# Linear attention beside a Mish layer: the two softmax planes of a head laid side by side, the queries' minus plane weighted before the product with kv, softmax sums on GpSimd, and an order of steps written as a list

## The chip, the cores and the metric

The kernel runs on one core of one Trainium2 chip. The metric is device time in microseconds (us) of one execution, the median of several runs, and lower is better. Inside a core five engines run their own instruction streams and wait for each other by semaphores: TensorE (PE, matrix products; its weight loads are listed apart as PEld), VectorE (DVE), ScalarE (ACT), GpSimd (POOL) and SyncE (SP, which here issues most DMAs). Products land in PSUM, which is eight banks of 128 partitions by 512 fp32 numbers; everything else lies in SBUF. GpSimd works on SBUF only in this kernel.

## The reference, cut to what matters

```python
x = A_x                                  # (1, 2048, 512) bf16
xn = layernorm(x)
q, k, v = split(xn @ wqkv)               # 32 heads of 16 columns each
pq, pk = q @ w_phi[head], k @ w_phi[head]
phi_q = concat(softmax(pq), softmax(-pq))    # over the 16 columns of a head: 32 columns
phi_k = concat(softmax(pk), softmax(-pk))
kv  = phi_k^T @ v                        # per head 32 x 16, summed over all 2048 rows
z   = sum over rows of phi_k             # per head 32
o   = (phi_q @ kv) / (phi_q @ z + 1e-6)
h   = xn @ w1 + b1                       # 512 -> 1792
out = x + o @ wo + mish(h) @ w2          # 1792 -> 512
```

The first softmax of a row is called the plus plane, the one of the negated logits the minus plane. No row maximum has to be kept: exp(p - max) and exp(min - p) are formed, and each plane's sum over its 16 columns divides it.

## The kernel before, in words

**Tiling.** The 2048 rows are 16 tiles of 128 rows, taken in 4 groups of 4 tiles. The Mish layer's hidden columns are 14 blocks of 128. `hidden` makes one unit: 4 matmuls of 512 columns (L178), then the Mish activation on ACT (L185); 14 units per group, 56 in all. `second_layer` (L400) makes 14 matmuls for one tile of 128 rows and leaves the sum open in PSUM; `project_out` (L409) adds 4 matmuls of o @ wo to the same sum; `residual` (L417) adds x on DVE and writes the tile out.

**The attention steps.** `fold` multiplies w_phi into the weights, so that `logits` (4 matmuls, L156) gives pk or pq directly. A stage s runs over one group: stages 0 to 3 are the keys of the four groups, stages 4 to 7 the queries. For each stage:

- `logits` makes the four tiles' logits, copied out of PSUM to `p_sb` by ACT or DVE (L196).
- `extremes` on DVE takes maximum and minimum over the 16 columns in a tree of four TENSOR_TENSOR instructions (L209 three times, L215), and subtracts (L220). It does so for the plus plane and then for the minus plane. The result is the tile `e`, of which there are two buffers.
- `exponentials` on ACT: exp over two of the four tiles at a time (L230).
- for the keys, `normalise` on DVE: TENSOR_REDUCE sums 16 columns (L248), RECIPROCAL (L256), a copy that doubles each factor (L257), and one multiplication of the whole of e (L261). Then `accumulate`: e^T @ [v, 1] on TensorE, 32 matmuls per group with 129 columns each (L284): a stationary block is one plane of 8 heads (128 columns), the moving one 128 columns of v and a column of ones.
- for the queries, e is turned by DMA (`turn`) without being normalised, and `attend` multiplies each plane with its masked kv: 8 matmuls of 144 columns per tile (L328), 128 columns of numerators, 8 of denominators and 8 of plain plane sums. ACT copies the result out of PSUM in four pieces (L337 to L344). `combine` on DVE (L360 to L385) then works out, from the two planes' sums and denominators, the factor of each plane, multiplies both planes' numerators (2048 columns for a pair of tiles), adds the two planes, and turns the result by DMA for `project_out`.

**The order.** The kernel is recorded under a manual schedule: each engine executes its instructions in the order in which the Python code issues them, and waits are put in where data or a buffer isn't ready. The order is written out by hand in the loops from L499 and from L567. SP issues nearly all DMAs in that order too, the transposes among them.

**LayerNorm** takes statistics on DVE (L116, L118) and the power -1/2 on POOL (L119, L122). The application (L128) runs on DVE for groups 0 and 1 and on POOL for groups 2 and 3.

**PSUM** has five banks for all products of 512 columns (`ps`), and three for one tile that holds kv or an `attend` result in turn (`ps2`).

The lines that the steps of the prediction rest on:

```python
rhs=vext[g % 2][:, i, j, 0:129]            # L287, accumulate
rhs=kvm[:, pl, j, :]                               # L331, attend, 144 columns
engine = nc.gpsimd if t0 > TPG else nc.vector      # L126, ln_apply
ps  = ctx.enter_context(tc.tile_pool(name="ps", bufs=5, ...))    # L59
```

Of the kernel before, what the change touches and what calls it, by code (L numbers as in the profile page):

```python
# [9 lines left out]
FP32 = mybir.dt.float32  # L10
# [3 lines left out]
AX = mybir.AxisListType  # L14


@with_exitstack
def kernel(
# [40 lines left out]
    ps = ctx.enter_context(tc.tile_pool(name="ps", bufs=5, space=bass.MemoryType.PSUM))  # L59
# [5 lines left out]
    kvm = persist.tile([P, 2, 4, 144], BF16, name="kvm")  # L65
# [14 lines left out]
    KVmask = consts.tile([P, 136], FP32, name="KVmask")  # L80
    vext = [vpool.tile([P, TPG, 4, 136], BF16, name=f"vext{i}") for i in range(2)]
# [11 lines left out]
    def fold(wT, dst, dve):  # L93

        for kt in range(KT):
            pf = ps.tile([P, 512], FP32, name="pfold", tag="mm")
            for j in range(4):
                nc.tensor.matmul(
                    pf[:, j * P : (j + 1) * P],
                    lhsT=wT[:, j, kt * P : (kt + 1) * P],  # L100
                    rhs=Wbd[:, j, :],
                    start=True,
                    stop=True,
                )
            if kt in dve:
                nc.vector.tensor_copy(dst[:, kt, :], pf[:])
            else:
                nc.scalar.copy(dst[:, kt, :], pf[:])
# [16 lines left out]
    def ln_apply(t0, n, mv, rstd, xn, at):  # L125
        engine = nc.gpsimd if t0 > TPG else nc.vector  # L126
        for i in range(n):
            engine.tensor_scalar(  # L128
                out=xn[:, at + i, :],
                in0=x_sb[:, t0 + i, :],  # L130
                scalar1=mv[:, i, 0:1],
                scalar2=rstd[:, i : i + 1],
                op0=ALU.subtract,
                op1=ALU.mult,
            )
# [26 lines left out]
    def value(t, copy):  # L162
        keep(t, project(wv, t), copy)

    def keep(t, pv, copy):
        copy(
            vext[(t // TPG) % 2][:, t % TPG, :, 0:128], pv.rearrange("p (j c) -> p j c", j=4)
        )

    units = iter([(g, f) for g in range(NG) for f in range(FT)])  # L170

    def hidden(n):

        for _ in range(n):
            g, f = next(units)
            ph = ps.tile([P, 512], FP32, name="ph", tag="mm")
            for kt in range(KT):
                nc.tensor.matmul(  # L178
                    ph[:],
                    lhsT=w1_sb[:, kt, f * P : (f + 1) * P],  # L180
                    rhs=xnT[:, g * TPG : (g + 1) * TPG, kt, :],
                    start=(kt == 0),
                    stop=(kt == KT - 1),
                )
            nc.scalar.activation(  # L185
                acts[:, f, g * 512 : (g + 1) * 512], ph[:], ACT.Mish, bias=b1f[:, f : f + 1]
            )
# [4 lines left out]
    def logits(s, i, copy):  # L192
        if i == 0:
            p_of[s] = smx.tile([P, TPG, 512], BF16, name="p_sb", bufs=1)
        pp = project(wkp if s < NG else wqp, (s % NG) * TPG + i)
        copy(p_of[s][:, i, :], pp)  # L196

    def extremes(s, between=None):

        e = epool.tile([P, TPG, 2, 512], BF16, name="e")  # L200
        e_of[s] = e
        pv = p_of.pop(s)[:].rearrange("p t (c e) -> p (t c) e", e=16)
        for pl, op in enumerate((ALU.max, ALU.min)):
            if pl == 1 and between is not None:
                between()
            src = pv
            for half in (8, 4, 2):
                m = smx.tile([P, 128, half], BF16, name=f"m{half}", bufs=1)
                nc.vector.tensor_tensor(  # L209
                    out=m[:], in0=src[:, :, 0:half], in1=src[:, :, half : 2 * half], op=op  # L210
                )
                src = m[:]

            m = smx.tile([P, 128, 1, 2], BF16, name="m1", bufs=1)
            nc.vector.tensor_tensor(out=m[:, :, 0, :], in0=src, in1=src[:, :, ::-1], op=op)  # L215
            mb = m[:].rearrange("p (t c) u o -> p t c u o", t=TPG).to_broadcast(
                [P, TPG, 32, 8, 2]
            )
            p5 = pv.rearrange("p (t c) (e o) -> p t c e o", t=TPG, o=2)
            nc.vector.tensor_tensor(  # L220
                out=e[:, :, pl, :].rearrange("p t (c e o) -> p t c e o", e=8, o=2),
                in0=p5 if pl == 0 else mb,
                in1=mb if pl == 0 else p5,
                op=ALU.subtract,
            )

    def exponentials(s, ks=(0, 1)):
        for k in ks:
            v = e_of[s][:, 2 * k : 2 * k + 2, :, :]
            nc.scalar.activation(v, v, ACT.Exp)  # L230
            if s >= NG:
                turn(s, k)

    def turn(s, k):

        qT = epool.tile([P, 2, 8, P], BF16, name="qT", bufs=3)
        qT_of[2 * (s - NG) + k] = qT
        for i in range(2):
            nc.sync.dma_start_transpose(
                out=qT[:, i, :, :],  # L240
                in_=e_of[s][:, 2 * k + i, :, :].rearrange("p l c -> p (l c)"),
            )

    def normalise(s, k, between=None):

        v = e_of[s][:, 2 * k : 2 * k + 2, :, :]
        t = smx.tile([P, 128], FP32, name="s")
        nc.vector.reduce_sum(  # L248
            t[:], v.rearrange("p t l (c e) -> p (t l c) e", e=16), axis=AX.X
        )  # L250
        if between is not None:
            between()
        r = smx.tile([P, 128], BF16, name="r")
        r2 = smx.tile([P, 128, 2], BF16, name="r2")
        with nc.allow_low_precision("the softmaxes are bf16"):
            nc.vector.reciprocal(r[:], t[:])  # L256
        nc.vector.tensor_copy(  # L257
            r2[:], r[:].rearrange("p (c o) -> p c o", o=1).to_broadcast([P, 128, 2])
        )
        vv = v.rearrange("p t l (c e o) -> p (t l c) e o", e=8, o=2)  # L260
        nc.vector.tensor_tensor(  # L261
            out=vv, in0=vv, in1=r2[:, :, None, :].to_broadcast([P, 128, 8, 2]), op=ALU.mult
        )

    def blocks(kv, pl, j, width):

        bank, at = (pl, j) if j < 3 else (2, pl)
        return kv[:, bank, at * 144 : at * 144 + width]

    def by_parts(kv, c0, c1):  # L270

        v = kv[:, :, 0:432].rearrange("p b (k c) -> p b k c", c=144)
        return v[:, 0:2, :, c0:c1], v[:, 2, 0:2, c0:c1]
# [3 lines left out]
    def accumulate(g):  # L277
        if g == 0:
            kv_of[0] = ps2.tile([P, 3, 512], FP32, name="pkv", tag="kv")
        e = e_of.pop(g)  # L280
        for j in range(4):
            for pl in range(2):
                for i in range(TPG):
                    nc.tensor.matmul(  # L284
                        blocks(kv_of[0], pl, j, 129),
                        lhsT=e[:, i, pl, j * P : (j + 1) * P],
                        rhs=vext[g % 2][:, i, j, 0:129],  # L287
                        start=(g == 0 and i == 0 and (j == 0 or (j == 3 and pl == 0))),
                        stop=(g == NG - 1 and i == TPG - 1),
                        skip_group_check=True,  # L290
                    )

    def mask_kv():
        a, b = by_parts(kv_of[0], 0, 128)
        nc.vector.tensor_tensor(
            out=kvm[:, :, 0:3, 0:128], in0=a,
            in1=KVmask[:, None, None, 0:128].to_broadcast([P, 2, 3, 128]), op=ALU.mult,
        )
        nc.vector.tensor_tensor(
            out=kvm[:, :, 3, 0:128], in0=b,  # L300
            in1=KVmask[:, None, 0:128].to_broadcast([P, 2, 128]), op=ALU.mult,
        )
        a, b = by_parts(kv_of[0], 128, 129)
        for pl in range(2):
            nc.vector.scalar_tensor_tensor(
                out=kvm[:, pl, 0:3, 128:136], in0=a[:, pl].to_broadcast([P, 3, 8]), scalar=5e-7,
                in1=KVmask[:, None, 128:136].to_broadcast([P, 3, 8]),
                op0=ALU.add, op1=ALU.mult,
            )
        nc.vector.scalar_tensor_tensor(  # L310
            out=kvm[:, :, 3, 128:136], in0=b.to_broadcast([P, 2, 8]), scalar=5e-7,
            in1=KVmask[:, None, 128:136].to_broadcast([P, 2, 8]), op0=ALU.add, op1=ALU.mult,
        )

    nd_of, oT_of, po_of, tmp_of = {}, {}, {}, {}

    def attend(h, i):

        if i == 0:
            nd_of[h] = (  # L320
                (wkp, wv)[h % 2][:].rearrange("p (i l) c -> p i l c", i=2),
                opool.tile([P, 2, 2, 2, 4, 8], FP32, name="ds"),
            )
        nm, ds = nd_of[h]
        pnd = ps2.tile([P, 3, 512], FP32, name="pnd", tag="kv")
        for pl in range(2):
            for j in range(4):
                nc.tensor.matmul(  # L328
                    blocks(pnd, pl, j, 144),
# [294 lines left out]
```

## Time and profile before

| | |
|---|---|
| time, median of 3 runs | 183.61 us (183.5 to 183.72) |
| span of the profiled execution, first to last instruction | 181.8 us; the page gives no time of its own for this execution beside the span |
| TensorE | busy 175.2 us (96%), 1024 matmuls, granted clock 1.00 |
| VectorE | busy 146.6 us (81%), 255 instructions |
| ScalarE | busy 126.3 us (69%), 194 instructions, 13 of them table loads of 1.283 us |
| GpSimd | busy 24.9 us (14%), nothing after 54.5 us |
| DMA | 18.02 MB, queue 1 busy for 40.5% of 16 engines' span |

How it is read: "busy" is the time in which an engine had an instruction running; a row of the groups gives line, engine, operation, tile names, shapes and a count, then busy us and mean ns of one, then the idle time just before and what ended it. The chain of work in order of time starts at the last instruction and goes back, at each step, to what released it; printed forwards it gives start, length and what ran. On that chain TensorE stands for 73%, VectorE for 18%. Lengths in the chain are from start to start, so they are the price of an instruction in a full stream, where the mean ns of a group also holds what overlaps the next instruction.

### The profile page before, as it was taken

The page shows a single profiled execution, that of the slowest core. Times are in us where ns is not written, and L with a number is a line of the kernel's source. Part 1 is how long each engine was busy: PE and PEld are TensorE (multiplying, and loading weights), DVE is VectorE, ACT ScalarE, POOL GpSimd, SP SyncE. Part 2 cuts the span into 40 slices and gives each one's busy share as a digit, 9 for nine tenths or more (in the row PEclk, how much of TensorE's full clock was granted, in tenths as well). Part 3 has the DMA queues.
Part 4 walks back from the last instruction along what each step waited for, and adds up shares of the span by engine and source line. Part 5 has one row for each costly group of instructions (what it writes and reads, how often), then busy time and mean ns, then how long its engine had stood idle before and what let it go on. Part 6 is the DMA issues. An engine that isn't in the chain of part 4 may idle for free.

```text
span 181.8 us, 2744 instructions
## 1 busy us (share of the span) xinstructions
PE 175.2 (96%) x1024; PEld 90.1 (50%) x1039; DVE 146.6 (81%) x255; ACT 126.3 (69%) x194; POOL 24.9 (14%) x30
## 2 busy tenths in 40 slices
PE   6899999999899999999999999999999999999993
PEld 2454344464344654644464555555554545455561
DVE  2989979999999799989998883399916997647963
ACT  2367999988998899979978999272842557235300
POOL 4403079301990000000000000000000000000000
PEclk9999999999999999999999999999999999999999
DMA  6997896300027100000001903933079302990633
GB/s 146 293 401 263 179 356 157 60 4 2 0 58 153 24 0 0 0 0 4 0 0 27 192 16 60 190 96 63 0 171 204 87 5 42 200 192 30 73 104 115
DMA packets 44393, 18.02 MB, mean 99 GB/s; under 512 B 36828, under 2 KB 43868, under 8 KB 44380
## 3 DMA queue, kind: packets, MB, share of 16 engines
q1 hardware_dynamic: 43408, 17.50, 40.5%
q10 hardware_dynamic: 972, 0.35, 0.7%
q8 instruction: 8, 0.13, 0.3%
q14 instruction: 5, 0.04, 0.1%
HBM read 6.84 MB, written 2.10 MB: 49 GB/s over the span
## 4 chain that ended last, share of the span: by engine, by line
PE 73%; DVE 18%; ACT 3%; issue 2%; DMA 2%; DVEq 0%
PE po L400 26%; PE ph L178 17%; PE pproj L156 14%; PE po L409 7%; PE pnd L328 4%; DVE stats L116 4%; PE pkv L284 3%; DVE m L209 3%; DVE s L248 2%; ACT e L230 2%; DVE e L220 2%; DMA x_sb<-in_A_x_dram 2%; DVE e L261 2%; DVE xn L128 1%; DVE r L256 1%
## 5 line engine op out<-in xcount | busy, mean ns | idle before, releaser
L400 PE MATMUL po<-w_sb,acts 128*128 128x512 bf16 (+1 forms) x232 | 50.0, 366 | 0.3
L178 PE MATMUL ph<-xnT,w_sb 128*128 128x512 bf16 x224 | 49.5, 379 | 0.6 <-ACT p_sb L196 0.6
L185 ACT ACTIVATE acts<-ph,b1f 128x512 bf16<-128x512 f32 x56 | 35.2, 696 | 2.6 <-PE ph L178 2.5
L178 PEld LDWEIGHTS <-w_sb 128*128 128x128 bf16 x224 | 21.8, 98 | 26.8 <-issue 0.9
L230 ACT ACTIVATE e<-e 128x2048 bf16<-128x2048 bf16 x16 | 30.1, 1906 | 6.7 <-DVE e L220 6.6
L400 PEld LDWEIGHTS <-acts 128*128 128x128 bf16 x238 | 22.9, 98 | 22.2
L156 PEld LDWEIGHTS <-xnT 128*128 128x128 bf16 x192 | 18.3, 98 | 21.6 <-DMA xnT<-xn 0.8
L417 DVE TENSOR_TENSOR x_sb<-po,x_sb 128x512 bf16<-128x512 f32 (+1 forms) x17 | 10.6, 654 | 12.6 <-PE po L409 12.6
L196 ACT CAST p_sb<-pproj 128x512 bf16<-128x512 f32 x25 | 14.0, 586 | 9.6 <-PE pproj L156 9.6
L248 DVE TENSOR_REDUCE s<-e 128x128 f32<-128x2048 bf16 x8 | 18.2, 2275 | 1.9 <-ACT e L230 1.9
L128 POOL TENSOR_SCALAR xn<-x_sb,mv,rstd 128x512 bf16<-128x512 bf16 x8 | 16.6, 2086 | 0.2
L156 PE MATMUL pproj<-wv,xnT 128*128 128x512 bf16 x62 | 14.8, 379 | 0.1
L156 PE MATMUL pproj<-wqk,xnT 128*128 128x512 bf16 x63 | 14.4, 379 | 0.1
L409 PE MATMUL po<-wqk,ob 128*128 128x512 bf16 (+1 forms) x65 | 14.3, 366 | 0.1
L337 ACT CAST wkp<-pnd 128x768 bf16<-128x768 f32 x8 | 6.4, 804 | 10.5 <-PE pnd L328 6.5
L209 DVE TENSOR_TENSOR m<-m 128x512 bf16<-128x512 bf16 (+1 forms) x32 | 11.5, 359 | 1.1
L156 PE MATMUL pproj<-wkp,xnT 128*128 128x512 bf16 x49 | 11.7, 379 | 0.1
L209 DVE TENSOR_TENSOR m<-p_sb 128x1024 bf16<-128x1024 bf16 x16 | 11.0, 685 | 1.0 <-ACT p_sb L196 1.0
L337 ACT CAST wv<-pnd 128x768 bf16<-128x768 f32 x8 | 6.4, 794 | 7.3 <-PE pnd L328 5.1
L328 PEld LDWEIGHTS <-qT 128*128 128x128 bf16 x128 | 9.1, 98 | 3.8
L116 DVE BATCH_NORM_STATS2 stats<-x_sb 128x6 f32<-128x512 bf16 x16 | 10.0, 678 | 1.2 <-DMA x_sb<-in_A_x_dram 1.2
L261 DVE TENSOR_TENSOR e<-e,r 128x2048 bf16<-128x2048 bf16 x8 | 10.7, 1337 | 0.3
(67 smaller groups left out, 179.4 us busy)
## 6 DMA issues: line engine op xcount, KB each, us to landing
w_sb<-in_B_w_dram SPq DMA_DIRECT2D x2, 1792.0 KB, 8.6
out_dram<-x_sb SPq DMA_DIRECT2D x15, 128.0 KB, 1.8
x_sb<-in_A_x_dram SPq DMA_DIRECT2D x1, 1024.0 KB, 11.4
x_sb<-in_A_x_dram SPq DMA_DIRECT2D x1, 512.0 KB, 3.9
wv<-in_A_wqkv_dram SPq DMA_DIRECT2D x1, 512.0 KB, 4.7
wqk<-in_A_wo_dram SPq DMA_DIRECT2D x1, 512.0 KB
x_sb<-in_A_x_dram SPq DMA_DIRECT2D x1, 256.0 KB, 3.2
x_sb<-in_A_x_dram ACTq DMA_DIRECT2D x1, 256.0 KB, 3.5
```

The source lines that it names most:

```text
L116: nc.vector.bn_stats(stats[:, i, :], x_sb[:, t0 + i, :])
L128: engine.tensor_scalar(out=xn[:, at + i, :], in0=x_sb[:, t0 + i, :], scalar1=mv[:, i, 0:1], scalar2=rstd[:, i : i + 1], op0=ALU.subtract, ...
L156: nc.tensor.matmul(pp, lhsT=xnT[:, t, kt, :], rhs=w[:, kt, :], start=(kt == 0), stop=(kt == KT - 1),)
L178: nc.tensor.matmul(ph[:], lhsT=w1_sb[:, kt, f * P : (f + 1) * P], rhs=xnT[:, g * TPG : (g + 1) * TPG, kt, :], start=(kt == 0), stop=(kt == ...
L185: nc.scalar.activation(acts[:, f, g * 512 : (g + 1) * 512], ph[:], ACT.Mish, bias=b1f[:, f : f + 1])
L209: nc.vector.tensor_tensor(out=m[:], in0=src[:, :, 0:half], in1=src[:, :, half : 2 * half], op=op)
L230: nc.scalar.activation(v, v, ACT.Exp)
L248: nc.vector.reduce_sum(t[:], v.rearrange("p t l (c e) -> p (t l c) e", e=16), axis=AX.X)
L261: nc.vector.tensor_tensor(out=vv, in0=vv, in1=r2[:, :, None, :].to_broadcast([P, 128, 8, 2]), op=ALU.mult)
L328: nc.tensor.matmul(blocks(pnd, pl, j, 144), lhsT=qT_of[h][:, i, pl * 4 + j, :], rhs=kvm[:, pl, j, :], start=True, stop=True,)
L400: nc.tensor.matmul(po[:, c], lhsT=acts[:, f, t * P : (t + 1) * P], rhs=w2_sb[:, f, c], start=(f == 0), stop=False,)
L409: nc.tensor.matmul(po[:, c], lhsT=oT_of[h][:, t % 2 * 4 + j, :], rhs=wo_sb[:, j, c], start=False, stop=(j == 3),)
```

## The change

Five things change at once, and the head (everything up to the logits of the first group) stays but for the names.

1. **Planes side by side.** The tile e is now [tile, 8 blocks, 2 planes, 64 columns]. A block is 4 heads, with both planes: 2 x 4 x 16 = 128 rows for the product. The moving operand of `accumulate` is then 64 columns of v and a column of ones, 65 in all, where there were 129; that of `attend` is 64 numerators and 4 denominators, 68 where there were 144. The number of matmuls is unchanged. One product now sums over both planes.
2. **The minus plane weighted first** (`weigh`, for the queries). So that one product can sum both planes, the minus plane is multiplied by (sum of the plus plane) / (sum of the minus plane) ahead of the DMA that turns e. Numerator and denominator then carry the same factor. `combine` shrinks to a reciprocal, a doubling copy and one multiplication of 1024 columns, and the four copies out of PSUM become two (`gather`).
3. **Sums on GpSimd** (`sums`). Fifteen of sixteen half-stages (two tiles each) are summed by four additions on GpSimd, over 1024, 512, 256 and 128 columns, with fp32 between. The eight of the queries are new, as the queries had no sums of their own; one of these (S 6 0) is a TENSOR_REDUCE on DVE. In three places GpSimd also makes the doubling copy.
4. **LayerNorm's application** runs on DVE for all groups.
5. **A new order**, written as a list of steps that the code executes one by one, with copies out of PSUM separated from the product that they empty, and with DVE (v), ACT (a) or GpSimd (p) named for each. PSUM is six banks for the products and two for kv or `attend`.

In the list: LN statistics, AP apply and turn (two tiles), L / LC logits and their copy, WL logits into the wide PSUM tile, V / VC values and copy, H / M hidden unit and Mish, E a plane of extremes, X exponentials, S sums, R reciprocal and doubling, N normalise, A accumulate (two tiles), KV mask, W weigh and turn, Q attend, G gather, C combine, O second layer, P project out, Y residual, F / FC fold and copy, LD late weight loads, WT the turned query weights.

```diff
+STEPS = """
+LN 1; V 0; V 2; H 0; VC 2 a; H 1; M 0; M 1; H 2; H 3; H 4; M 2; H 5; H 6; M 3; M 4; M 5; E 0 0; E 0
+1; M 6; H 7; H 8; M 7; H 9; H 10; M 8; M 9; AP 1 0; H 11; H 12; H 13; M 10; M 11; M 12; M 13; AP 1
+1; LN 2; LN 3; V 1; L 1 0; VC 0 v; WL 1; X 0 0; V 3; L 1 3; VC 1 a; H 14; AP 2 0; AP 2 1; X 0 1; AP
+3 0; S 0 0 p; LC 1 0 v; LC 1 3 a; V 5; VC 3 a; LC 1 1 v; H 15; M 14; AP 3 1; WL 2; M 15; VC 5 a; LC
+1 2 v; E 1 0; H 16; H 17; V 4; M 16; M 17; H 18; M 18; H 19; M 19; H 20; H 21; M 20; M 21; VC 4 v; S
+0 1 p; H 22; H 23; M 22; M 23; E 1 1; R 0 0 p; V 7; VC 7 v; X 1 0; V 6; L 2 0; LD; L 2 3; WT; R 0 1
+v; L 2 2; S 1 0 p; LC 2 0 v; LC 2 3 a; L 2 1; LC 2 2 a; X 1 1; F 0; FC 0 a; S 1 1 p; H 24; M 24; VC
+6 v; H 25; N 0 0; H 26; H 27; N 0 1; A 0 0; H 28; A 0 1; H 29; M 25; M 26; M 27; H 30; M 28; LC 2 1
+v; E 2 0; F 1; H 31; M 29; V 11; R 1 0 p; M 30; E 2 1; M 31; H 32; M 32; L 3 0; F 2; X 2 1; S 2 1 p;
...
+VC 14 a; LC 5 2 a; LC 5 1 a; X 4 1; L 5 3; LC 5 3 v; L 6 1; A 3 0; A 3 1; E 5 0; S 4 1 p; H 49; H
+50; M 49; M 50; H 51; M 51; H 52; H 53; H 54; M 52; W 4 0; E 5 1; M 53; M 54; L 6 0; O 1; KV; X 5 0;
+Q 0 0; G 0 0; L 6 3; LC 6 0 a; LC 6 1 v; H 55; W 4 1; LC 6 2 v; Q 0 1; G 0 1; C 0; O 2; O 3; LC 6 3
...
+3; P 6; P 7; S 6 1 p; W 6 1; Q 5 0; S 7 0 p; Y 5; W 7 0; O 11; G 5 0; Y 6; Y 7; Q 5 1; O 12; G 5 1;
+Q 6 0; O 13; C 4; C 5; G 6 0; Q 6 1; P 8; P 9; S 7 1 p; G 6 1; W 7 1; Q 7 0; P 10; Y 8; Y 9; Y 10; C
+6; P 11; G 7 0; Q 7 1; G 7 1; O 14; O 15; P 12; P 13; C 7; P 14; Y 11; Y 12; Y 13; Y 14; P 15; Y 15
+"""
...
-    ps = ctx.enter_context(tc.tile_pool(name="ps", bufs=5, space=bass.MemoryType.PSUM))
+    ps = ctx.enter_context(tc.tile_pool(name="ps", bufs=6, space=bass.MemoryType.PSUM))
...
-        engine = nc.gpsimd if t0 > TPG else nc.vector
+        engine = nc.vector
...
+    def sums(s, k, pooled=False):
+
+        t = smx.tile([P, 128], FP32, name="s")
+        s_of[s, k] = t
+        src = pair(s, k).rearrange("p t j l (c e) -> p (t j l c) e", e=16)
+        if not pooled:
+            nc.vector.reduce_sum(t[:], src, axis=AX.X)
+            return
+        for half in (8, 4, 2, 1):
+            h = smx.tile([P, 128, half], FP32, name=f"h{half}", bufs=1)[:] if half > 1 else t[:, :, None]
+            nc.gpsimd.tensor_tensor(
+                out=h, in0=src[:, :, 0:half], in1=src[:, :, half : 2 * half], op=ALU.add
+            )
+            src = h
...
+    def weigh(s, k):
+
+        t = s_of.pop((s, k))[:].rearrange("p (t l c) -> p t l c", l=2, c=4)
+        r = smx.tile([P, 16, 4], FP32, name="q")
+        r2 = smx.tile([P, 16, 4, 2], BF16, name="q2")
+        nc.vector.reciprocal(r[:], t[:, :, 1, :])
+        nc.vector.tensor_tensor(
+            out=r2[:], in0=t[:, :, 0, :, None].to_broadcast([P, 16, 4, 2]),
+            in1=r[:, :, :, None].to_broadcast([P, 16, 4, 2]), op=ALU.mult,
+        )
+        vv = pair(s, k).rearrange("p t j l c -> p (t j) l c")[:, :, 1, :].rearrange(
+            "p t (c e o) -> p t c e o", e=8, o=2
+        )
+        nc.vector.tensor_tensor(
+            out=vv, in0=vv, in1=r2[:, :, :, None, :].to_broadcast([P, 16, 4, 8, 2]), op=ALU.mult
+        )
+        turn(s, k)
...
+                    blocks(kv_of[0], j, 65),
+                    lhsT=e[:, i, j, :, :].rearrange("p l c -> p (l c)"),
+                    rhs=vext[g % 2][:, i, j, 0:65],
...
+                blocks(pnd, j, 68), lhsT=qT_of[h][:, i, j, :], rhs=kvm[:, j, :],
...
+    for step in STEPS.split(";"):
+        name, *args = step.split()
+        run[name](*(int(a) if a.isdigit() else a for a in args))
```

More of the change, by code (lines that the diff above doesn't have):

```diff
@@ L160, in project, with value, keep @@
         return pp
-    def value(t, copy):
-        keep(t, project(wv, t), copy)
-    def keep(t, pv, copy):
+    pv_of, ph_of, pl_of = {}, {}, {}
+    def value(t):
+        pv_of[t] = project(wv, t)
+    def keep(t, copy):
         copy(
-            vext[(t // TPG) % 2][:, t % TPG, :, 0:128], pv.rearrange("p (j c) -> p j c", j=4)
-        )
[L170 to L186, printed above, removed]
-            )
+            vext[(t // TPG) % 2][:, t % TPG, :, 0:64],
+            pv_of.pop(t).rearrange("p (j c) -> p j c", j=8),
+        )
@@ L190, with logits, take @@
     p_of, e_of, qT_of = {}, {}, {}
-    def logits(s, i, copy):
+    def logits(s, i, pp=None):
+        pl_of[s, i] = project(wkp if s < NG else wqp, (s % NG) * TPG + i, pp)
+    def take(s, i, copy):
         if i == 0:
             p_of[s] = smx.tile([P, TPG, 512], BF16, name="p_sb", bufs=1)
[L195 to L217, printed above, removed]
-            )
[L219 to L225, printed above, removed]
@@ L275 @@
-    kv_of = {}
[L277 to L291, printed above, removed]
@@ L471 @@
     ln_apply(0, 2, *st0, xn, 0)
-    fold(wT, wkp, (3,))
+    for kt in range(KT):
+        fold(wT, kt)
+        unfold(wkp, kt, (act, act, act, dve)[kt])
     ln_turn_pe(0, xn, 0, dve)
@@ L477 @@
     ln_apply(2, 2, *st1, xn, 2)
-    logits(0, 0, act)
+    logits(0, 0)
+    take(0, 0, act)
     for i in range(2, 4):
@@ L548 @@
[L548 to L593 removed]
+        logits(0, i)
@@ new lines, with wide @@
+    wide_of = {}
+    def wide(i):
+        if i == 1:
+            wide_of[0] = ps2.tile([P, 2, 512], FP32, name="pwide", tag="kv")
+        logits(1, i, wide_of[0][:, i - 1, :])
+    wT_of = {}
+    run = {
+        "LN": stats, "AP": apply, "LD": load_late, "WL": wide,
+        "L": logits, "LC": lambda s, i, c: take(s, i, copies[c]),
+        "V": value, "VC": lambda t, c: keep(t, copies[c]),
+        "H": hidden, "M": mish,
+        "E": extremes, "X": exponentials, "S": lambda s, k, c: sums(s, k, c == "p"),
+        "R": lambda s, k, c: invert(s, k, c == "p"), "N": normalise, "A": accumulate,
+        "KV": mask_kv, "W": weigh, "Q": attend, "G": gather, "C": combine,
+        "O": second_layer, "P": project_out, "Y": residual,
+        "WT": lambda: wT_of.update({0: load_turned(0)}),
+        "F": lambda kt: fold(wT_of[0], kt), "FC": lambda kt, c: unfold(wqp, kt, copies[c]),
+    }
```

395 lines of the change are left out of this document (162 added, 233 removed).

## The prediction

> **What bounds the kernel now.** I read the page's engine list first, then the waits of TensorE, then the chain of waits in order of time, then the groups with shapes kept apart.
>
> The engine list:
>
> ```profile
> PE 175.2 (96%) x1024; PEld 90.1 (50%) x1039; DVE 146.6 (81%) x255; ACT 126.3 (69%) x194; POOL 24.9 (14%) x30
> ```
>
> TensorE has work for nearly the whole span, and the waits view shows that it hardly ever waits once started:
>
> ```profile
> PE warm L457 <- POOL ident masks.py:199: 1.4, 1, 1.4
> PE ph L178 <- ACT p_sb L196: 0.6, 1, 0.6
> PE ptr L140 <- DVE wkp L106: 0.5, 1, 0.5
> ```
>
> The chain in order of time (start, length, what) gives the price of each kind of product in a full stream:
>
> ```profile
> 58.95 1.81 PE pkv L284 x32
> ...
> 67.67 0.89 PE pfold L98 x16
> ...
> 84.19 8.63 PE ph L178 x40
> ...
> 102.84 0.50 PE pnd L328 x8
> ```
>
> A product of 512 columns costs 0.2158 us (8.63/40), of 129 columns 0.0566 (1.81/32), of 128 columns 0.0556 (0.89/16), of 144 columns 0.0625 (0.50/8). So from 8.5 us to 177.8 us the kernel is a gapless stream of products; what shortens it is fewer TensorE nanoseconds, provided no other engine is late.
>
> The last view is the timeline of DVE and POOL where LayerNorm runs on POOL beside DVE's normalise (each POOL instruction is 2.08 us, the lines merge two):
>
> ```profile
> 29.36 4.16 POOL L128 TENSOR_SCALAR xn<-x_sb,mv,rstd 128x512 bf16<-128x512 bf16 x2
> ...
> 29.56 1.67 DVE L261 TENSOR_TENSOR e<-e,r 128x2048 bf16<-128x2048 bf16 x1
> ```
>
> ```profile
> 50.32 4.13 POOL L128 TENSOR_SCALAR xn<-x_sb,mv,rstd 128x512 bf16<-128x512 bf16 x2
> ...
> 53.64 1.23 DVE L261 TENSOR_TENSOR e<-e,r 128x2048 bf16<-128x2048 bf16 x1
> ```
>
> The same DVE multiplication takes 1.23 us where it starts 1.2 us into a POOL instruction, and 1.67 where it starts 0.2 us after one began (the same at 48.42, behind the POOL start at 48.22). POOL's own time doesn't move. DVE loses 0.44 us to POOL's start, about until POOL has read its 512 columns (0.64 us).
>
> **Narrower products.** 128 matmuls of 129 columns become 65, 128 of 144 become 68; before, 128 x 0.0566 + 128 x 0.0625 = 15.24 us. Low end: the straight line through 512 and 129 columns is 0.4157 ns per column plus 3.0 ns, so 30.0 and 31.2 ns, 7.83 us, 7.4 saved. High end: nothing is gained below the narrowest row, 55.6 ns each, 14.23 us, 1.0 saved (each product needs its own weight load, which no row shows alone in a stream). The rows at 128, 129, 144 and 512 columns lie on one line with no sign of a floor, so I take the line plus 8 ns for weight loads no longer fully covered: 38.5 ns, 9.86 us, **5.4 saved**. All other products stay in number and width.
>
> The Trainium skill ("TensorE: Matmul & The Clock Gate", section "Back-to-back issue gap") gives N/2.4 + 2.5 ns, but says that it leaves out the weight load. By it the saving would be 7.5 us and the time 179.5; the four rows above agree with it to 0.4 ns, and nothing here shows 65 columns.
>
> **The head's end.** Due times from here on are the rows' lengths added along the list, from the end of the first logits at 12.87 us. The list puts two values (V 0, V 2) ahead of the first hidden unit, where there were four. So H 0 is due at 12.87 + 8 x 0.2158 = 14.6; w1's load is issued at 5.9 and lands 9.1 us later, at 15.0. **+0.4**. X 0 0 moves back by some 6 us (before 22.84; now behind 14 Mish units, due 28.7), and the whole of the keys' softmax with it; that is covered by group 0's hidden units, which now all stand ahead. SP: w2 and wo are issued behind six xnT transposes instead of two (about 32.5 instead of 20.1), the turned query weights behind these; with 8.2 us for w2 and 4.7 for a turned load they land at about 45, and F 0 is due at 47.8, O 0 at 87. Nothing.
>
> **ACT.** Copies of `attend`: before 0.80 + 0.38 + 0.26 + 0.22 = 1.66 us per tile, now 0.22 + 0.59: 16 x 0.85 = -13.6. Seven logits copies, the wide copy of 1.43, a value and two folds go to DVE, about -7. Two more table loads, +2.6. ACT falls to about 108 us. No gain of its own, as it wasn't the bound.
>
> **DVE.** Off: seven of eight sums of 2.275 us, -15.9; `combine` from 29.7 (its rows added) to 8 x (0.553 + 0.226 + 0.692) = 11.8, -17.9; three doublings, -1.0; kv's mask, about -0.9. On: 8 `weigh` at 0.553 + 0.292 + 0.692, +12.3; LayerNorm's other 8 tiles at 0.343, +2.7; 13 more copies out of PSUM at 0.68, +8.8. Net -12, to about 135 us. The total is no problem; the place is.
>
> **POOL.** It loses 16.6 us of LayerNorm and gets 15 sums of 1920 columns. No row has an addition there. Low end from the 128-column memset, 0.205 us, 1.6 ns per column, 3.1 us a sum; high end from TENSOR_SCALAR, 2.086/512 = 4.07 ns, 7.8 us. Nearest to small plain work are the selects, 293 and 344 ns for 128 columns, so 2.5 ns: **4.8 us a sum**, 72 in all. A TENSOR_REDUCE is done in 2.3, so each softmax is 2.5 us later; the list leaves room for that, as A s stands far behind X s.
>
> **What is late next: DVE between E 1 0 and E 5 1.** E 1 0 can start at 35.3 (WL 2 made and copied), as TensorE ends WL 2 at 34.9. DVE's steps from there to E 5 1 add up to 60.8 us: ten planes of extremes at 2.97, eight N at 1.25, the rest copies, reciprocals and one W. E 5 1 is due at 105.6: it releases X 5 0 (1.82), behind which on ACT stands G 0 0 (0.75), which empties PSUM for Q 0 1, due on TensorE at 108.2. So 105.6 - 35.3 - 60.8 = 9.5 us of room. But e has two buffers: E 2 0, E 3 0, E 4 0 and E 5 0 wait until A 0 1, A 1 1, A 2 1 and A 3 1 have run on TensorE, and what is lost behind such a wait isn't won back before it. I count 6 of the 9.5 as useful.
>
> Into this stretch fall eight sums, 32 POOL additions. Two-input work (planes and N, 40 of 60.8 us) takes two thirds of DVE's time, so about 20 additions meet it. Bounds for one meeting: 0, as at 53.64, and 1.2 us, a whole addition (4.8/4). I take the measured 0.44: 8.8 us, less 6, **+3 us** of TensorE waiting, mostly where ACT's exponentials hold up copies behind them (VC 8 behind X 2 0, LC 4 2 behind X 3 0). If POOL were free of cost, 0; if 1.2, 24 less at most 9.5: 14.5.
>
> **Behind E 5 1** DVE has some 50 us of work in 70 and is led by TensorE. W ahead of `turn` adds a sum and 1.6 us between exp and the turned queries; S 5 1 to Q 3 0 has 128.7 - 115.2 = 13.5 us for 4.8 + 1.6 + about 4 of SP and DMA. Last, Q 7 1 ends some 7.8 us before P 14, and G, C 7 and its transpose take 0.8 + 1.6 + 1.2 + 3.1 = 6.7: covered by 1 us. Behind the last product nothing changes.
>
> **The sum.** -5.4 + 0.4 + 3.0 = -2.0. The span of 181.8 becomes 179.8. The timed runs have 183.61 as median, 1.8 above the profiled span; I leave that as it is: **181.6 us**.
>
> **Rivals.**
>
> *A. DVE and POOL shut each other out.* Place: the stretch above. If every two-input DVE instruction waits for the whole of the addition that it meets, TensorE loses 14.5 to 18 us: 183.6 - 5.0 + 14.5 to 18 = 193 to 197, I say 194. It decides from (5.0 + 6)/20 = 0.55 us a meeting, barely above the 0.44 seen. For it: POOL read 512 columns in 0.64 us, an addition reads twice its columns, so the first of a sum would read for 2.6 us. Against it: the instruction at 29.56 did not wait out the 1.88 us that POOL's had left.
>
> The Trainium skill ("SBUF — State Buffer", section "Who interferes with whom") says that a VectorE instruction with two SBUF inputs and a GpSimd one that reads SBUF exclude each other for a whole instruction. By that rule this rival is the outcome. The trace agrees that they meet, and not on the length: 1.67 us where the rule would make it 3.1.
>
> *B. Narrow products are no cheaper than 128 columns.* 1.0 saved: 183.6 - 1.0 + 0.4 + 3.0 = 186.0. For it: one weight load of 98 ns per product; against it: the line.
>
> *C. POOL is dear, 7.8 us a sum.* Then S 4 1 ends near 109, W 4 1 and LC 6 2 behind it release O 2 some 2.7 us late, and A 3 1, P 2 and Q 3 0 lose about 2.5 more: 181.6 + 3 to 5 = 185.
>
> *D. Nothing collides*: 183.6 - 5.4 + 0.4 = 178.6, and 176.6 with the line's full saving.
>
> **How the numbers follow.** Forecast and D together, one mechanism with meetings from 0 to 0.55 us, 0.51, own range 176.6 to 183.5; A 0.30; B 0.11; C 0.08. A measurement tells 0.2% (0.37 us) from no change. Of the 0.51, 0.49 are faster and 0.02 the same; of B and C 0.02 the same; the rest, 0.47, slower, and I put 0.01 of that at the same for A's lower edge. Range 176.6 to 194: outside are A's upper half and a little below.
>
> **What would show it.** The products of 65 and 68 columns in the chain: 38 ns (30 to 56). The waits of TensorE: near zero outside 50 to 110 us, about 3 us inside, ended by ACT. POOL's rows of L296: 2.5, 1.3, 0.6, 0.3 us. The planes' rows on DVE (685, 425, 292, 292, 1225 ns before): means up by a few tens of ns in the forecast, by hundreds in A. X 5 0 at about 105. The forecast is wrong if DVE's two-input means double, or if narrow products show more than 50 ns.

## The result, and the profile after

The changed kernel takes 196.87 us (median of 4 runs, 196.23 to 197.38), the kernel before 183.67 in the same session. The ratio is 1.0711, 95% interval 1.0683 to 1.0739: 13.2 us slower. The forecast of 181.6 us was wrong in sign and the time lies above the range's upper end of 194.0. It is what rival A gives (193 to 197).

The engine list of the changed kernel, and three rows of its 40 slices (busy tenths; PEclk is the granted clock in tenths):

```profile
PE 173.2 (89%) x1023; PEld 83.9 (43%) x1039; DVE 167.5 (86%) x247; ACT 113.2 (58%) x153; POOL 88.1 (45%) x85
...
PE   7899999999699989785996993999499999799993
...
DVE  2989993799999999999998999699999999992814
...
PEclk9999999999789999999999997899999999999999
```

TensorE is busy 2 us less than before in a span 12.7 us longer (194.5 against 181.8). DVE was forecast at 135 us and shows 167.5. The granted clock falls twice, each time at a gap in the PE row; at the other gaps it stays. The chain that ended last has turned over. Before, TensorE had 73% of it and VectorE 18%; now:

```profile
DVE 56%; PE 31%; ACT 6%; issue 4%; DMA 2%; POOL 0%; DVEq 0%; POOLq 0%; ACTq 0%
```

POOL holds 0% of that chain, and DVE waited for a sum of POOL's only once, for 0.4 us. So it is not POOL's sums that come late. The groups of DVE with shapes kept apart (count, busy us, mean ns of one, then idle time) show where the 32 us went:

```profile
L248 DVE TENSOR_TENSOR m<-p_sb 128x1024 bf16<-128x1024 bf16 x16 | 16.2, 1012 | 0.4
L257 DVE TENSOR_TENSOR e<-p_sb,m 128x2048 bf16<-128x2048 bf16 x8 | 12.4, 1544 | 0.6
L248 DVE TENSOR_TENSOR m<-m 128x512 bf16<-128x512 bf16 x16 | 11.8, 736 | 0.6
...
L248 DVE TENSOR_TENSOR m<-m 128x256 bf16<-128x256 bf16 x16 | 10.3, 642 | 0.6
...
L257 DVE TENSOR_TENSOR e<-m,p_sb 128x2048 bf16<-128x2048 bf16 x8 | 9.8, 1225 | 0.3
...
L237 DVE CAST p_sb<-pproj 128x512 bf16<-128x512 f32 x11 | 7.5, 682 | 0.6 <-PE pproj L192 0.6
```

The same operations took 685, 1225, 425, 292, 1225 and 676 ns before. The four rows shown that grew all read two inputs in SBUF, and each grew by 311 to 350 ns. The second subtraction (e<-m,p_sb) did not, but it never meets an addition: in this order it always starts with POOL idle. Copies out of PSUM did not grow either, and they do meet: one at 49.82, beside an addition begun at 49.83, took 0.68 us.

One place in the timeline shows the mechanism. POOL's additions and DVE's tree at the start of the prediction's stretch (start, length, instruction; x2 merges two):

```profile
35.73 2.64 POOL L296 TENSOR_TENSOR h<-e 128x1024 f32<-128x1024 bf16 x1
38.45 2.03 POOL L296 TENSOR_TENSOR h<-h 128x512 f32<-128x512 f32 x2
```

```profile
35.70 0.69 DVE L248 TENSOR_TENSOR m<-p_sb 128x1024 bf16<-128x1024 bf16 x1
36.42 3.51 DVE L248 TENSOR_TENSOR m<-m 128x512 bf16<-128x512 bf16 x2
```

DVE started first, at 35.70, and ran its usual 0.69 us; POOL's addition, started 0.03 us later, took 2.64 us instead of the 2.13 it takes alone (at 31.12). Then DVE's next instruction waited until that addition was over: in the chain it stands with 2.24 us, where it needs 0.43. So the engines wait for each other to the end of the instruction, whichever came first. The rest of the trace agrees: 48 DVE instructions are longer by more than 0.05 us than the same rows of the run without sums (e2, below), and in each the extra time is what the POOL instruction running at its start had left, less 0.13 to 0.15 us. In 47 of the 48 that POOL instruction is an addition, in one a copy.

The waits of TensorE, its wait at the very start left out:

```profile
PE pnd L387 <- DVE kvm L373: 3.1, 1, 3.1
PE po L442 <- ACT p_sb L237: 2.6, 1, 2.6
PE ph L214 <- DVE p_sb L237: 2.3, 1, 2.3
PE pkv L356 <- DVE e L317: 2.3, 1, 2.3
PE pproj L192 <- ACT p_sb L237: 1.9, 1, 1.9
...
PE pnd L387 <- DMA qT<-e: 1.2, 1, 1.2
```

These six are 13.4 us, where the kernel before had 1.1 behind its start. Three end on a DVE step and two on a copy of ScalarE.

### The profile page after: what moved, and what is told of

Same layout as the page of the kernel before. It is cut to its first block, busy times and chain, and to the rows that moved or that the text cites. A ratio compares the mean times of both kernels' runs of the same rounds, so it can differ in the third digit from the quotient of the medians.

```text
span 194.5 us, 2775 instructions
## 1 busy us (share of the span) xinstructions
PE 173.2 (89%) x1023; PEld 83.9 (43%) x1039; DVE 167.5 (86%) x247; ACT 113.2 (58%) x153; POOL 88.1 (45%) x85
## 4 chain that ended last, share of the span: by engine, by line
DVE 56%; PE 31%; ACT 6%; issue 4%; DMA 2%; POOL 0%; DVEq 0%; POOLq 0%; ACTq 0%
DVE m L248 18%; DVE e L257 10%; PE ph L214 8%; PE po L442 8%; PE pproj L192 6%; DVE m L254 4%; PE po L450 3%; DVE e L335 3%; ACT e L272 3%; PE warm L496 3%; DVE q L328 3%; DVE p_sb L237 2%; DVE r L309 2%; DVE x_sb L458 2%; DVE e L317 2%
## 5 line engine op out<-in xcount | busy, mean ns | idle before, releaser
L214 PE MATMUL ph<-xnT,w_sb 128*128 128x512 bf16 x224 | 53.6, 390 | 3.2 <-DVE p_sb L237 2.3
L296 POOL TENSOR_TENSOR h<-e 128x1024 f32<-128x1024 bf16 x15 | 33.4, 2226 | 45.5 <-ACT e L272 31.5
L296 POOL TENSOR_TENSOR h<-h 128x512 f32<-128x512 f32 (+1 forms) x30 | 34.4, 1147 | 2.4
L192 PEld LDWEIGHTS <-xnT 128*128 128x128 bf16 x192 | 18.6, 99 | 25.9 <-issue 4.7
L248 DVE TENSOR_TENSOR m<-m 128x512 bf16<-128x512 bf16 (+1 forms) x32 | 22.0, 689 | 1.1
L458 DVE TENSOR_TENSOR x_sb<-po,x_sb 128x512 bf16<-128x512 f32 (+1 forms) x17 | 10.7, 653 | 8.5 <-PE po L450 8.5
L248 DVE TENSOR_TENSOR m<-p_sb 128x1024 bf16<-128x1024 bf16 x16 | 16.2, 1012 | 0.4
L237 ACT CAST p_sb<-pproj 128x512 bf16<-128x512 f32 x19 | 10.8, 587 | 8.1 <-PE pproj L192 4.3
L450 PE MATMUL po<-wqk,oT 128*128 128x512 bf16 (+1 forms) x65 | 14.7, 366 | 0.2
L401 ACT COPY ds<-pnd 128x32 f32<-128x32 f32 x16 | 2.9, 184 | 18.8 <-PE pnd L387 18.8
L192 PE MATMUL pproj<-wkp,xnT 128*128 128x512 bf16 x55 | 13.2, 379 | 0.2 <-DVE xnT L179 0.2
L257 DVE TENSOR_TENSOR e<-p_sb,m 128x2048 bf16<-128x2048 bf16 x8 | 12.4, 1544 | 0.6
L296 POOL TENSOR_TENSOR s<-h 128x128 f32<-128x128 f32 x15 | 10.8, 717 | 1.2
```

The source lines that it names most:

```text
L192: nc.tensor.matmul(pp, lhsT=xnT[:, t, kt, :], rhs=w[:, kt, :], start=(kt == 0), stop=(kt == KT - 1),)
L214: nc.tensor.matmul(ph_of[u][:], lhsT=w1_sb[:, kt, f * P : (f + 1) * P], rhs=xnT[:, g * TPG : (g + 1) * TPG, kt, :], start=(kt == 0), stop= ...
L237: copy(p_of[s][:, i, :], pl_of.pop((s, i)))
L248: nc.vector.tensor_tensor(out=m[:], in0=src[:, :, 0:half], in1=src[:, :, half : 2 * half], op=op)
L257: nc.vector.tensor_tensor(out=e_of[s][:].rearrange("p t j l c -> p (t j) l c")[:, :, pl, :].rearrange("p t (c e o) -> p t c e o", e=8, o=2 ...
L296: nc.gpsimd.tensor_tensor(out=h, in0=src[:, :, 0:half], in1=src[:, :, half : 2 * half], op=ALU.add)
```

## The experiments

Three theories of the loss. **P**: POOL's additions shut out DVE's instructions. **L**: the sums on POOL come too late, by their length of 4.65 us. **O**: the new order is too tight in itself. A2 and A1, further on, split P. e1, e2, e4, e5 and e7 leave softmax sums out, so their output is not the kernel's; they show time alone.

| kernel | us | ratio to before | 95% interval |
|---|---|---|---|
| changed kernel | 196.87 | 1.0711 | 1.0683 to 1.0739 |
| e1_memset: fills for sums | 177.28 | 0.9657 | 0.9641 to 0.9673 |
| e2_nosum: no sums | 176.06 | 0.9591 | 0.9577 to 0.9606 |
| e3_dve_sums: sums on DVE | 195.49 | 1.0651 | 1.0631 to 1.067 |
| e4_keys_add: additions for keys only | 188.23 | 1.0251 | 1.0228 to 1.0275 |
| e5_queries_add: additions for queries only | 184.92 | 1.0064 | 1.0042 to 1.0085 |
| e7_one_source: TENSOR_SCALAR for sums | 176.47 | 0.9616 | 0.9602 to 0.9631 |
| e8_bf16_adds: additions in bf16 | 194.92 | 1.0602 | 1.0575 to 1.0629 |
| v3: order by hand, sums on DVE and POOL | 186.68 | 1.0144 | 1.0104 to 1.0184 |
| v5: the same, no additions on POOL | 180.26 | 0.9819 | 0.9805 to 0.9834 |

### Does POOL's time or POOL's reading cost? (e1_memset, e2_nosum)

```diff
-        for half in (8, 4, 2, 1):
-            h = smx.tile([P, 128, half], FP32, ...)
-            nc.gpsimd.tensor_tensor(out=h, in0=src[:, :, 0:half], in1=src[:, :, half : 2 * half], op=ALU.add)
-            src = h
+        nc.gpsimd.tensor_copy(idle[:, 0:2], pair(s, k)[:, 0, 0, 0, 0:2])
+        for n in (2560, 1300, 860):              # e1 only; e2 leaves these out
+            nc.gpsimd.memset(idle[:, 0:n], 0.0)
+        nc.gpsimd.memset(t[:], 8.0)
```

> The kernel after, but each GpSimd sum is replaced by work of the same length that reads almost nothing: one copy of two columns of e (so that it still waits for exp), three fills of 2560, 1300 and 860 columns, and a fill of the sums with 8.0. The softmaxes' sums are left out. Theory P (port): DVE instructions with two SBUF inputs wait out GpSimd's additions; with nothing read, the waits go, DVE's busy time falls from 167.5 us to about 132, TensorE's stalls nearly vanish, and the time is 177 to 180 us. Rival L (late sums): a sum on GpSimd comes 2.3 us later than on DVE and holds up the chain exp, sum, accumulate; GpSimd is as late as before, so 193 to 197 us. Rival O (the order is too tight for DVE whatever GpSimd does): 190 us or more.

> The kernel after, with each GpSimd sum replaced by a copy of two columns and one fill of the sums with 8.0, so GpSimd is neither late nor reading. The softmaxes' sums are left out. P: 176 to 179 us, at most 1.5 us under the run with long fills. L: 176 to 179 us too, but then 15 us or more under the run with long fills. O: 190 us or more.

Measured 177.28 and 176.06 us. The groups of e1, and its slices of the granted clock:

```profile
L248 DVE TENSOR_TENSOR m<-p_sb 128x1024 bf16<-128x1024 bf16 x16 | 10.9, 682 | 0.4
...
L248 DVE TENSOR_TENSOR m<-m 128x512 bf16<-128x512 bf16 x16 | 6.8, 426 | 0.6
```

```profile
PEclk9999999999999999999999999999999999999999
```

With POOL busy 82.7 us (88.1 in the changed kernel), with the same steps in the same order and the same tile of e waited for, 19.6 us are gone and every two-input row of DVE is back at its length of before. Against L: the fills keep the sums' length. Against O: the order itself runs at 176 to 177. What remains is that POOL's additions read SBUF and fills do not.

### Is POOL then better than DVE for the sums? (e3_dve_sums)

All sixteen sums become `reduce_sum` on DVE, each directly ahead of its R or W, and the three doublings return to DVE (all `p` in the list become `v`).

> The kernel after, with all sixteen sums as TENSOR_REDUCE on DVE, each put straight ahead of the reciprocal that needs it, and all doublings on DVE. P: no waits for GpSimd, but 15 x 2.28 = 34 us more DVE work, against 36 us of waiting that go, so DVE is as busy as in the kernel after (165 us) and the time is about as long, 190 to 197 us. L: the sums come sooner, so 182 to 187 us. The two-column excess of DVE's rows (for instance the 512-column row of L248 at 736 ns) is back at 425 ns in either case.

Measured 195.49 us, 1.4 us less than the changed kernel and inside P's 190 to 197. The engine list:

```profile
PE 174.9 (90%) x1039; PEld 84.1 (43%) x1039; DVE 166.4 (86%) x265; ACT 114.5 (59%) x153; POOL 8.3 (4%) x22
```

DVE's busy time is 166.4 against 167.5 us. Without sums (e2) it is 132.1, so moving them to POOL swapped 34.3 us of sums and doublings on DVE for 35.4 us of being shut out. This order has no room for either.

### Where is it lost? (e4_keys_add, e5_queries_add)

```diff
     def sums(s, k, pooled=False):
...
+        if s >= NG:                              # e5: s < NG
+            h = smx.tile([P, 128, 8], FP32, name="h8", bufs=1)
+            nc.gpsimd.tensor_copy(h[:, 0, 0:2], pair(s, k)[:, 0, 0, 0, 0:2])
+            for _ in range(4):
+                nc.gpsimd.memset(h[:], 0.0)
+            nc.gpsimd.memset(h[:, 0:40, :], 0.0)
+            nc.gpsimd.memset(t[:], 8.0)
+            return
```

> The changed kernel with the real additions on GpSimd for the keys alone; the queries' sums are replaced by a copy of two columns and write-only fills of the same length (5 fills and one of s), so the queries' weights are left out. Place of the loss, theory K (it is lost in the keys' stretch, as the prediction had it): VectorE's block from E 1 0 to E 5 1 took 84 us in the changed kernel (35 to 119) and 70 us in the kernel with fills alone (35 to 105), so 14 of the 19.6 us are lost there: 177.3 + 14 = 191. Rival theory T (it is lost in the tail, where W holds up the transposes that attend waits for): 177.3 + 5 = 182 or less.

> The reverse: the real additions on GpSimd for the queries alone, the keys' sums replaced by the copy and the fills (the keys' softmax sums are left out). Theory K: 177.3 + 5 = 182, 181 to 185. Theory T: 191 or more. If the two losses are independent, this run's loss and that of the kernel with the keys' additions add up to 19.6 us over 177.3.

Measured 188.23 and 184.92 us. Over e1's 177.28 the keys' additions cost 10.9 us and the queries' 7.6, together 18.6 of 19.6. So the losses add up, and neither K (14 and 5) nor T (5 and 14) had the split: it is K's way round and more even (e5 lies at the upper end of K's 181 to 185, e4 2.8 us under K's 191). The last subtraction of E 5 1 tells how late the stretch ends; in e1, e4, e5 and the changed kernel, in this order:

```profile
103.26 1.22 DVE L257 TENSOR_TENSOR e<-m,p_sb 128x2048 bf16<-128x2048 bf16 x1
```

```profile
113.92 1.23 DVE L257 TENSOR_TENSOR e<-m,p_sb 128x2048 bf16<-128x2048 bf16 x1
```

```profile
106.76 1.23 DVE L257 TENSOR_TENSOR e<-m,p_sb 128x2048 bf16<-128x2048 bf16 x1
```

```profile
118.07 1.23 DVE L257 TENSOR_TENSOR e<-m,p_sb 128x2048 bf16<-128x2048 bf16 x1
```

The keys delay it by 10.7 us, which is nearly all that they cost. The two sums of the queries that fall ahead of E 5 1 delay it by 3.5, and the other 4.1 of the queries' 7.6 us are lost behind it. In the changed kernel the delay is 14.8, and 19.6 - 14.8 = 4.8 are lost behind it.

### Which reading shuts DVE out? (e7_one_source, e8_bf16_adds)

The 0.44 us of the prediction came from a TENSOR_SCALAR, one tile read, bf16 to bf16; the additions read two, and write f32. The first edit puts that very operation in place of the additions, the second makes the additions' tiles bf16:

```diff
-        for half in (8, 4, 2, 1):
...
+        flat = pair(s, k).rearrange("p t j l c -> p (t j l c)")
+        for c in (0, 512):
+            nc.gpsimd.tensor_scalar(
+                out=idle[:], in0=flat[:, c : c + 512], scalar1=mhalf[:, 0:1],
+                scalar2=mhalf[:, 1:2], op0=ALU.subtract, op1=ALU.mult,
+            )
+        nc.gpsimd.memset(t[:], 8.0)
```

```diff
-            h = smx.tile([P, 128, half], FP32, name=f"h{half}", bufs=1)[:] if half > 1 else t[:, :, None]
+            h = smx.tile([P, 128, half], BF16, name=f"h{half}", bufs=1)[:] if half > 1 else t[:, :, None]
```

> Each GpSimd sum replaced by two TENSOR_SCALAR of 128x512, the same operation as LayerNorm's in the kernel before (2.09 us each there, 4.2 us together, near the additions' 4.65), reading e, and a fill of s; so the sums are left out. Theory A2 (what shuts VectorE out is an instruction with two tiles read, and one with one tile read lets go early, as in the 0.44 us that the prediction took): 178 to 181. Rival theory A1 (any GpSimd instruction that reads a tile shuts it out for its whole length): 30 x 2.09 = 63 us of such reading against the 75 us of the additions, so 0.8 of the loss or more: 193 or above.

> The changed kernel with the intermediate tiles of the GpSimd sums in bf16 instead of f32; the four additions, their two sources and everything else stay. Theory A2 (two tiles read at once shut VectorE out, whatever their type): as the changed kernel, 191 to 199. Rival theory A3 (f32 on GpSimd is what shuts VectorE out; the one-source operation that did not was bf16 to bf16): 176 to 180, and then this version beats both kernels.

Measured 176.47 and 194.92 us. Both rivals fall: 73 us of POOL reading one tile at a time cost next to nothing (0.4 us over e2, and 176.47 is even under A2's 178), and the additions cost nearly the same in bf16. DVE's busy time did grow by 6.3 us in e7 (138.4 against 132.1 in e2), which this order had room for. The timeline of e7 at the same place as above, POOL and then DVE:

```profile
35.51 4.37 POOL L297 TENSOR_SCALAR idle<-e,mhalf 128x512 bf16<-128x512 bf16 x2
...
35.65 1.16 DVE L248 TENSOR_TENSOR m<-p_sb 128x1024 bf16<-128x1024 bf16 x1
```

DVE's 0.685 become 1.16, 0.47 more, though POOL goes on for another 3 us: the prediction's 0.44, found again. And POOL pays for its part of the meetings, as its group shows:

```profile
L297 POOL TENSOR_SCALAR idle<-e,mhalf 128x512 bf16<-128x512 bf16 x30 | 72.9, 2431 | 37.5 <-ACT e L272 25.2
```

On average it takes 2431 ns, where it was 2086 for LayerNorm in the kernel before. What a TENSOR_SCALAR costs DVE is regular too: the 16 two-input lines that one holds up in e7 go on 1.45 to 1.46 us before its end, while a CAST of 128 columns (at 109.06) goes on only 0.15 us before it. In e8 the tree's first row on DVE is 1184 ns, longer still than the changed kernel's 1012.

So additions hold DVE to their end and a TENSOR_SCALAR of one tile does not, as A2 has it. That the number of tiles makes the difference is not shown. The two also differ in how much they read (the first addition 2048 columns in 2.13 us, a TENSOR_SCALAR 512 in 2.09) and in the pattern of the columns. And every kernel here has a POOL instruction with two tiles that does not hold DVE: LayerNorm's power, on four columns. In the changed kernel, POOL and then DVE:

```profile
14.60 1.17 POOL L158 TENSOR_TENSOR rstd<-rstd,mhalf 128x4 f32<-128x4 f32 x1
```

```profile
14.45 0.75 DVE L248 TENSOR_TENSOR m<-m 128x512 bf16<-128x512 bf16 x2
15.24 0.29 DVE L254 TENSOR_TENSOR m<-m 128x256 bf16<-128x256 bf16 x1
15.56 1.23 DVE L257 TENSOR_TENSOR e<-p_sb,m 128x2048 bf16<-128x2048 bf16 x1
```

All these DVE lines have their usual lengths. A wait that lasts only while POOL is still reading would fit all three cases, but no view shows POOL's reads, and no run here varies the number of columns and of tiles apart.

### A version that uses this (v3, v5)

Both keep the narrow products, planes side by side and `weigh`. The keys' steps go back to the order of the kernel before, LayerNorm of groups 2 and 3 to POOL, and the sums to DVE as a tree. v3 leaves the last three sums of the queries on POOL.

```diff
-        engine = nc.vector
+        engine = nc.gpsimd if t0 >= 2 * TPG else nc.vector
...
-            nc.vector.reduce_sum(t[:], src, axis=AX.X)
+            with nc.allow_low_precision("the softmaxes are bf16"):
+                for half in (8, 4, 2, 1):
+                    h = smx.tile([P, 128, half], BF16, name=f"m{half}", bufs=1)[:] if half > 1 else t[:, :, None]
+                    nc.vector.tensor_tensor(out=h, in0=src[:, :, 0:half], in1=src[:, :, half : 2 * half], op=ALU.add)
+                    src = h
```

> The narrow products and the planes side by side of the changed kernel with the steps in the order of the kernel before for the keys; key sums on VectorE as a tree of four additions in bf16 (0.69 + 0.43 + 0.29 + 0.29 = 1.69 us by the rows of the maxima of the kernel before, against 2.28 us for the reduction); LayerNorm of groups 2 and 3 on GpSimd as before; queries' sums as the tree too, but for the last three, which stay on GpSimd. If the shut-out by additions is the whole loss: the kernel before less 7.0 us on the narrow products, 176.6; with 2 to 4 us lost to a tail that is written out by hand: 177 to 181. If the new order or the layout costs something in itself: 184 or above.

v3 took 186.68 us, which is in the branch "184 or above": the new order costs more than the 2 to 4 us allowed for the tail written out by hand. TensorE waited 5.0 us in two places, `pnd` for the copy out of the one bank of `attend` (nm), which stood on ScalarE behind exponentials that themselves waited for DVE. In the first place no POOL addition had run yet; in the second, DVE's tree of E 7 1 stood beside POOL's S 6 1 and took 2.62 us for its first line, usually 0.69. The clock fell to 6 tenths:

```profile
PEclk9999999999999999999999999999669987999999
```

v5 orders the tail anew and takes POOL's last three sums away:

```diff
-1 v; W 5 1; E 6 1; O 5; X 6 0; Q 2 0; G 2 0; O 6; P 2; P 3; Q 2 1; G 2 1; C 2; ...
+1 v; W 5 1; E 6 1; O 5; Q 2 0; G 2 0; O 6; P 2; P 3; Q 2 1; G 2 1; X 6 0; C 2; ...
...
-C 3; X 7 0; S 7 0 p; X 7 1; S 7 1 p; Q 4 0; G 4 0; W 6 1; O 9; ...
+S 6 1 v; W 6 1; Q 4 0; G 4 0; X 7 0; O 9; Q 4 1; G 4 1; X 7 1; O 10; C 4; ... S 7 0 v; W 7 0; ...
```

> The version before this with all sums as trees on VectorE (nothing of two tiles is left on GpSimd behind the head) and the tail's order mended where TensorE waited: the copies that free the bank of attend stand ahead of X 6 0, X 7 0 and X 7 1 on ScalarE. In the version before, TensorE waited 2.4 + 0.7 + 2.6 us there, and its clock was 0.82 from 130 to 155 by the slices, some 4 us more. If that was all: 186.7 less 5.7 less 4 = 177, range 175 to 180. If the new order makes stalls of its own: 180 to 187.

Measured 180.26 us (180.18 to 180.5), 3.4 us (1.8%) under the kernel before and 16.6 under the changed one. The engine list:

```profile
PE 169.6 (95%) x1039; PEld 82.8 (46%) x1039; DVE 149.1 (83%) x291; ACT 116.2 (65%) x165; POOL 26.7 (15%) x30
```

It is 3 us above the 177 expected and just above the range of 175 to 180; TensorE still waits 1.6 us for one residual and 1.2 for two transposes. As two things changed at once, it isn't shown which of them brought how much.

## Why the prediction was wrong

**The price of one meeting** is the step that failed, "I take the measured 0.44". Measured: DVE's busy time from 35 us to 119 us, where E 5 1 ends (119.30), is 81.0 us in the changed kernel, against 60.8 of steps by the prediction's count; e2, without sums, shows 58.4 up to the end of its own E 5 1 (103.36). The windows of the changed kernel (length, then PE, PEld, DVE, ACT and POOL busy):

```profile
35.00:119.00 84.00, 73.28 (x442) 34.78 (x446) 80.99 (x91) 59.91 (x74) 51.26 (x41) 0.98 0.15 38
```

So more than 20 us were lost by being shut out, where 8.8 were entered. Row by row against e2, 33 DVE instructions of this stretch are longer, by 0.07 to 1.80 us and 0.71 on average, 23.5 us in all. Thirty of them have two inputs; three are doubling copies in SBUF (4.1 us), which the prediction had not counted as meeting anything. So both factors were too small, 0.44 us for the price and about 20 for the number. One reason for the number is in the list of steps: it has nine sums between E 1 0 and E 5 1 (S 0 1 to S 4 1), 36 additions, where the prediction entered eight and 32.

The row that 0.44 came from was read rightly (e7 has 0.47 for the same), but it belongs to an operation that lets go after less than a third of its length (begun 0.14 us before DVE's line in e7, which then lost 0.47 of the 1.95 us that were left). An addition does not let go before its last 0.15 us (2.24 us for a line of 0.43). The upper bound, 1.2 us for each of 20 meetings and 24 us in all, was near the 23.5. The prediction had named a possible reason, twice the columns read, and placed the limit at 0.55 us; that its 0.44 us is POOL's time for reading 512 columns is an inference that no run here tests.

The Trainium skill ("SBUF — State Buffer", section "Who interferes with whom") has DVE work with two SBUF inputs and a GpSimd instruction that reads SBUF exclude each other for a whole instruction, and a GpSimd instruction that only writes not. For additions and fills the runs agree (2.24 us of wait; 682 ns beside fills). For TENSOR_SCALAR they do not: 1.16 us in e7, where the wait for the whole instruction would have made some 2.6. Nor do they for the power of four columns, beside which DVE's lines kept their lengths. There the measurement decides.

**The place and the room** were right. Without sums E 5 1 ends at 103.36 (forecast 105.6). In the changed kernel it ends 15.9 us later than that, while DVE's busy time up to it is 22.9 us longer (81.3 against 58.4), so 7.0 us of the room took up losses; 6 were entered.

**"Behind E 5 1 DVE is led by TensorE"** was the second miss: 4.8 us are lost there (19.6 - 14.8, against e1; 4.1 in e5), where additions also meet `weigh` (1112 ns instead of 692) and its small product (918 instead of 292), which stand ahead of the turned queries. The waits `po <- ACT p_sb` (at 136) and `pnd <- DMA qT` (at 166) lie in this part.

**Narrower products**: right in direction, short in size. On the timeline of the changed kernel 32 products of 65 columns fill the 1.02 us between two starts, and eight of 68 the 0.25 to 0.26 us:

```profile
106.89 1.18 PE L356 MATMUL pkv<-vext,e 128*128 128x65 bf16 x32
107.91 5.34 PE L214 MATMUL ph<-xnT,w_sb 128*128 128x512 bf16 x24
...
170.89 0.42 PE L387 MATMUL pnd<-kvm,qT 128*128 128x68 bf16 x8
171.14 3.18 PE L442 MATMUL po<-w_sb,acts 128*128 128x512 bf16 x14
```

1.02/32 is 31.9 ns, against 30.0 by the straight line and the 38.5 taken. 256 x 32 ns = 8.2, so 7.0 us are saved and not 5.4. The 8 ns for weight loads were not there, and rival B falls. The estimate of 7.5 us by the formula of the Trainium skill ("TensorE: Matmul & The Clock Gate", section "Back-to-back issue gap") was nearer.

**Right**: the head's end (TensorE's weight loads wait 0.5 us for w1, 0.4 entered); POOL's sums (4.65 us alone at 31.12, 4.8 taken), so that rival C falls; DVE's own work (132.1 us in e2, about 135 forecast); nothing from the late loads of w2 and wo. ACT, forecast at about 108 us, shows 113.2, but did not bound the kernel.

**The sum** with the measured terms: 183.6 - 7.0 + 0.5 = 177.1, near e1's 177.3 and e2's 176.1. The changed kernel's 196.9 is 19.6 above e1: 14.8 up to the end of E 5 1, and 4.8 as the remainder, so this second step is no check of its own. Of the 18.7 us between the spans of e1 and the changed kernel, 4.3 are TensorE's busy time (173.2 against 168.9). A part of this is a lower clock behind two of the waits: 16 products from 50.55, at a granted clock of 0.67, took 5.14 us where 3.45 are usual, and from 120.20 to 124.00 the granted clock was 0.63. Behind the waits that end at 90.17, 105.17 and 138.70 (2.3, 1.9 and 2.6 us) it stayed at 1.00.

## What to carry to other kernels

Before work moves from VectorE to GpSimd, list what both read from SBUF. Here GpSimd's additions of two tiles and VectorE instructions that read two tiles ran one after the other, so the move freed nothing. Fills cost such work nothing, a TENSOR_SCALAR of one tile under 0.5 us each time, and a power of four columns nothing. A measured price belongs to the operation that it was measured on; where the new one differs in just the respect that the mechanism turns on, take the whole instruction as the price until a run says otherwise. Where one engine's busy time grows without new work, compare the mean of the same row in both profiles before looking for a late transfer.

## What the runs showed that was not expected

- Fills on POOL leave two-input work on DVE alone, but not a plain copy: in e1 the doubling COPY of 256 bf16 columns took 907 ns on average, 311 in e2, and the doubling CAST 378 against 227. DVE's busy time is 4.1 us longer in e1 than in e2 for it, and that is nearly all of the runs' difference in DVE rows. The same copy waits for additions too: 2.00 us at 47.91, to the end of an addition begun at 47.63. The Trainium skill ("SBUF — State Buffer", section "Who interferes with whom") names copies among the instructions that can take the ports shared with GpSimd; these two rows agree.
- The exclusion goes both ways: POOL's sum of 4.65 us averages 5.24 in the changed kernel, and its last addition of 128 columns shows 1.26 us instead of 0.40 where DVE was at work.
- A product of 65 columns, each with a weight load of its own, costs 31.9 ns in a stream: no floor shows down to half the width that the kernel before had.
